# Linear attention and a GELU feed-forward on one core: the first batch by half its heads

## The chip, the cores and the metric

The kernel runs on one core of one Trainium2 chip. A core has TensorE (matmuls, results in PSUM), VectorE, ScalarE (activation functions), GpSimd (called POOL in profiles) and SyncE (SP, which issues most of the transfers here), and 16 DMA engines that move data between HBM and SBUF. The metric is the device time of one execution in microseconds (us); lower is better.

## The reference

Linear attention over 8 batches, 8 heads, 576 positions and head size 64, then a feed-forward layer on the heads put side by side (4608 tokens of 512):

```python
def phi(x):
    return np.where(x > 0, x, np.exp(x) - 1.0) + 1.0
q_p, k_p = phi(q), phi(k)
kv = np.einsum('bhsd,bhse->bhde', k_p, v)
z = np.sum(k_p, axis=2)
num = np.einsum('bhsd,bhde->bhse', q_p, kv)
den = np.einsum('bhsd,bhd->bhs', q_p, z)[..., None] + 1e-06
attn = num / den
# x = attn, transposed to (4608, 512)
h = x @ w_in                                  # 512 -> 2048
g = 0.5 * h * (1.0 + np.tanh(c * (h + 0.044715 * h * h * h)))
out = g @ w_out                               # 2048 -> 512
```

Inputs and the output are float32; the matmuls work in bf16.

## The kernel before

**Tiles.** Of each batch's 576 rows, 512 (`MAIN`) form one tile of tokens, in four chunks c of 128; the remaining 64 rows (`REST`) of all batches form a ninth tile, which is computed last. One iteration j computes one tile of 512 tokens: 16 blocks m of h (`h_mm`, four matmuls of 128x512 each, into one PSUM bank, then GELU on ScalarE into g), and the output in four chunks t, each of 16 matmuls in four groups u of four blocks m (`o_mm`). These are 32 slots, and a hand-written plan (`fill`, `at`, `run`) says after which slot of which iteration the work on a later batch stands. Iteration 0 goes through u in the outer loop, so that the quarters of w_out, which are still arriving, are needed one after the other: slots 16 to 19 need the first, 20 to 23 the second, 24 to 27 the third, 28 to 31 the fourth.

**Attention of one batch.** phi is max(x + 1, 1) ("linear", VectorE), limited by exp(x) (ScalarE; "least", a minimum on VectorE). v is cast into a tile with a column of ones behind each head (E = 65 columns), so that kv and z come from the same matmuls. Two heads make a block of kvbd, a block-diagonal tile of 128 rows and 130 columns. For each chunk of tokens, n = q_p times kvbd holds numerator and denominator; VectorE takes the reciprocal and multiplies, which gives x (`nab_evac`); x is transposed into xt. Batches 0 and 1 transpose on TensorE, later ones by DMA.

**The first batch** (`first_batch`, from line 377) stands ahead of iteration 0. Matmuls on a tile of zeros (`keep_warm`) fill TensorE's time during the loads. q is loaded in two halves by the parity of the head, k and v in halves of four heads (`halves`). Both halves of q, k and v go through phi and the casts, kv is computed in four banks and copied to kvbd by VectorE and ScalarE. Then each chunk c has n over all heads, in a pair of banks (`nab`, even chunks) or in two single banks (`nab_in_banks`, odd ones), the transpose, the copy of xt on ScalarE, and its quarter of the first three blocks m of h (`h_quarter`, 12 matmuls of 128x128). Block m = 3 follows as the first whole one.

**Batch 1** (`plan_second`) is woven into iteration 0: maps after slot 15, the transposes of q after 23, the casts of v after 25, kv after 26, then the n of its chunks after 27, 28, 29 and 30. In `kv`, VectorE first casts a part of the last quarter of w_out (line 484) and then copies kv into kvbd (line 290).

**Loads.** All loads of inputs and weights are issued by SP in one order: q, k, v of batch 0; the four pieces of w_in; then pieces of w_out and q, k, v of batch 1 in turn; then batch 2 (with the rest rows of k and v of batches 2 and 3, `load_rest`, line 118) and batch 3. Weights come as float32 and are cast to bf16, w_in and most of w_out by GpSimd. Loads use a pool of seven buffers (`pld`), and each transfer uses one of eight completion counters in turn, so a transfer is issued only when the eighth one before it has landed. PSUM has six single banks (`ps_b`) and one pair (`ps_a`).

```python
def load_w(wr, i):
    t = pld.tile([P, 4, 512], FP32, name="w_st", tag="ld")
    ...
    src = wr[:, :, 512 * i : 512 * (i + 1)] if wr is w_in_r else wr[:, 4 * i : 4 * i + 4, :]
    nc.sync.dma_start(out=t, in_=src)
```

A row of this piece of w_in is 512 float32, 2 KB in one run.

Of the kernel before, what the change touches and what calls it, by code (L numbers as in the profile page):

```python
# [15 lines left out]
def kernel(  # L16
# [6 lines left out]
    moe_w_out: bass.AP,  # L23
    out: bass.AP,
):

# [45 lines left out]
    def bank(name, shape, dt=FP32):  # L74
        return ps_b.tile(shape, dt, name=name, tag="b")
# [5 lines left out]

    ld = {}
    PAIRED = (0, 1)

    def ld_tile(name, b):
        shape = [P, NP, J * D] if b in PAIRED and name != "q" else [P, H, C * D]
# [3 lines left out]
        s = src[b].rearrange("h s d -> (h s d)").rearrange("(u n f) -> n u f", n=P, f=J * D)  # L90
        nc.sync.dma_start(out=ld[name, b][:, us, :], in_=s[:, us, :])  # L91

    def load_q_paired(b, parities=(0, 1)):
        src = q[b, :, 0:MAIN, :].rearrange("(u a) (p c) d -> p a u (c d)", a=2, c=C)
        for a in parities:
            nc.sync.dma_start(out=ld["q", b][:, NP * a : NP * (a + 1), :], in_=src[:, a])  # L96

    def load_main(name, src, b):
        ld_tile(name, b)
        nc.sync.dma_start(  # L100
            out=ld[name, b],
            in_=src[b, :, 0:MAIN, :].rearrange("h (p c) d -> p h (c d)", c=C),
        )

    def load_rest(name, src, m):
        t = (pqr if name == "qr" else prest).tile([P, H, D], FP32, name=name)
        ld[name, m] = t
        for s in range(2):
            r = t[REST * s : REST * (s + 1)]
            rows = src[2 * m + s, :, MAIN:S, :]  # L110
            if name == "qr" and m == 0:
                for a in range(2):
                    nc.sync.dma_start(
                        out=r[:, NP * a : NP * (a + 1), :],
                        in_=rows.rearrange("(u a) p d -> p a u d", a=2)[:, a],
                    )
            else:
                nc.sync.dma_start(out=r, in_=rows.rearrange("h p d -> p h d"))

# [10 lines left out]
    def load_w(wr, i):  # L130
        t = pld.tile([P, 4, 512], FP32, name="w_st", tag="ld")
        w_st[wr is w_in_r, i] = t
        src = wr[:, :, 512 * i : 512 * (i + 1)] if wr is w_in_r else wr[:, 4 * i : 4 * i + 4, :]
        nc.sync.dma_start(out=t, in_=src)

    def cast_w_in(i, fn, fs=slice(0, 512)):
        fn(
# [12 lines left out]
    for n in "qkv":  # L150
        ld_tile(n, 0)
    for s in range(2):
        load_q_paired(0, (s,))
        load_pairs("k", k, 0, halves[s])
    for s in range(2):
        load_pairs("v", v, 0, halves[s])
# [1 line left out]
        load_w(w_in_r, i)  # L158
    load_w(w_out_r, 0)
    ld_tile("q", 1)  # L160
    load_q_paired(1)
    load_w(w_out_r, 1)
    ld_tile("k", 1)
    load_pairs("k", k, 1)
# [127 lines left out]
    def nab_mm(qt_c, kvbd, ns, rows=slice(0, P)):  # L292
        for i in range(NP):
            nc.tensor.matmul(  # L294
                ns[i // 2][rows, 2 * E * (i % 2) : 2 * E * (i % 2 + 1)],
                lhsT=qt_c[:, i, rows],
                rhs=kvbd[:, i, :],
                skip_group_check=True,
            )

    def x_view(x, paired):
        return x.rearrange("p (u a d) -> p a u d" if paired else "p (a u d) -> p a u d", a=2, d=D)
# [16 lines left out]
        nab_mm(qt_c, kvbds[b % 4], [n_ps[:, a] for a in range(2)])  # L319
        return nab_evac(n_ps, b in PAIRED)  # L320

    def nab_in_banks(qt_c, b):
        ns = [bank("n_ps", [P, 4 * E]) for _ in range(2)]
        nab_mm(qt_c, kvbds[b % 4], ns)
        x = px.tile([P, d_model], BF16, name="x")
        for a in range(2):
            n_v = ns[a].rearrange("p (u e) -> p u e", e=E)
            r = psm.tile([P, NP], FP32, name="r1")
            nc.vector.reciprocal(r, n_v[:, :, D])
            nc.vector.tensor_tensor(  # L330
                x_view(x, b in PAIRED)[:, a],
                n_v[:, :, 0:D],
                r[:, :, None].to_broadcast([P, NP, D]),
                op=ALU.mult,
            )
        return x

    def transpose_x(x, xt_c, fn):
        t_ps = bank("t_ps", [P, NP, P], BF16)
        for i in range(NP):  # L340
            nc.tensor.transpose(t_ps[:, i, :], x[:, P * i : P * (i + 1)], ident)  # L341
        fn(out=xt_c, in_=t_ps)  # L342

    xts = {}
    qts = {}

    def h_mm(h_ps, xt, m, ts=slice(0, MAIN)):
        for c in range(KM):
            nc.tensor.matmul(  # L349
                h_ps[:, ts],  # L350
                lhsT=w_in_sb[:, c, P * m : P * (m + 1)],
                rhs=xt[:, c, ts],
                start=(c == 0),
                stop=(c == KM - 1),
                skip_group_check=True,
            )
# [20 lines left out]
    def first_batch():  # L377
        w_ps = bank("w_ps", [P, 512])

        def keep_warm(n):  # L380
            for _ in range(n):
                nc.tensor.matmul(w_ps, lhsT=warm[:, 0:P], rhs=warm)  # L382

        qt = pt.tile([P, C, NP, P], BF16, name="qt")
        qs = (slice(0, 4), slice(4, 8))

        def transpose_q(s, fn):
            t_ps = bank("t_ps", [P, C, 2, P], BF16)
            for i in range(2):
                for c in range(C):  # L390
                    h = 4 * s + 2 * i
                    nc.tensor.transpose(
                        t_ps[:, c, i, :], phi["q", 0][:, c, h : h + 2, :], ident
                    )
            fn(out=qt[:, :, 2 * s : 2 * s + 2, :], in_=t_ps)

        keep_warm(18)
        for s in range(2):
            for n, hs in (("q", qs[s]), ("k", halves[s])):
                exp_of(n, 0, hs)  # L400
                linear_of(n, 0, hs)
                least_of(n, 0, hs)
        transpose_q(0, nc.scalar.copy)
        keep_warm(10)
        transpose_q(1, nc.scalar.copy)
        keep_warm(2)
        for ii in range(2):
            cast_v_paired(0, halves[ii], nc.vector.tensor_copy)
        for ii in range(2):
            kv_ps = [bank("kv_ps", [P, E]) for _ in range(2)]  # L410
            kv_paired(0, ii, lambda a, ii: kv_ps[a])
            for a, fn in enumerate((nc.vector.tensor_copy, nc.scalar.copy)):
                block = slice(2 * a + ii, 2 * a + ii + 1)
                kv_evac(0, block, kv_ps[a].rearrange("p (i e) -> p i e", i=1), fn)
        gelu_table()
        for s in range(2):
            cast_w_in(0, nc.gpsimd.tensor_copy, slice(256 * s, 256 * s + 256))
        for i in range(1, 4):
            cast_w_in(i, nc.gpsimd.tensor_copy)
        for i in range(2):  # L420
            cast_w_out(i, nc.gpsimd.tensor_copy)
        cast_w_out(2, nc.gpsimd.tensor_copy, slice(0, 2))
        keep_warm(2)

        xts[0] = pt.tile([P, NP, MAIN], BF16, name="xt")
        x = {0: nab(qt[:, 0], 0), 1: nab_in_banks(qt[:, 1], 0)}
        for c in range(C):
            transpose_x(x[c], xt_chunk(0, c), nc.scalar.copy)
            if c + 2 < C:
                x[c + 2] = (nab, nab_in_banks)[c % 2](qt[:, c + 2], 0)  # L430
            if c > 0:
                h_quarter(0, c - 1, 3)
        h_quarter(0, C - 1, 3)

    first_batch()

# [311 lines left out]
```

## Time and profile before

| | us |
|---|---|
| Median of 3 runs | 287.87 (287.83 to 287.99) |
| The profiled execution | 288.24 |
| Its span, first to last instruction | 286.2 |
| ScalarE's time in table loads, 16 of them | 20.6 |
| TensorE, o matmuls (L642) | 126.3 |
| TensorE, h matmuls (L349, main tiles) | 116.7 |
| Load of w_in, issue to landing, median of 4 pieces | 14.7 |
| Load of w_out, issue to landing, median of 4 pieces | 13.6 |

The span is what the trace covers; the rest of the execution's time lies around it. "Busy" is the time in which an engine had an instruction at work. The granted clock of TensorE was 0.998 of full speed over the span. A timeline line has the start, the duration, the engine, the source line, the operation with output and input, the count and, in brackets, how long the engine had been idle and what released it. The two largest rows of TensorE make 243 of its 276.6 busy us, and a matmul of 128x512 is issued every 0.216 us in an unbroken stream: four of them, one block m of h, take 0.864 us.

### The profile page before, as it was taken

The page shows a single profiled execution, that of the slowest core. Times are in us where ns is not written, and L with a number is a line of the kernel's source. Part 1 is how long each engine was busy: PE and PEld are TensorE (multiplying, and loading weights), DVE is VectorE, ACT ScalarE, POOL GpSimd, SP SyncE. Part 2 cuts the span into 40 slices and gives each one's busy share as a digit, 9 for nine tenths or more (in the row PEclk, how much of TensorE's full clock was granted, in tenths as well). Part 3 has the DMA queues.
Part 4 walks back from the last instruction along what each step waited for, and adds up shares of the span by engine and source line. Part 5 has one row for each costly group of instructions (what it writes and reads, how often), then busy time and mean ns, then how long its engine had stood idle before and what let it go on. Part 6 is the DMA issues. An engine that isn't in the chain of part 4 may idle for free.

```text
span 286.2 us, 4541 instructions
## 1 busy us (share of the span) xinstructions
PE 276.6 (97%) x1839; PEld 137.1 (48%) x1868; DVE 107.8 (38%) x180; ACT 164.8 (58%) x226; POOL 18.4 (6%) x25
## 2 busy tenths in 40 slices
PE   8789999999999999999999999999999999999994
PEld 3464456445455445544554455444544444444443
DVE  3840476634865472544246614640412010000011
ACT  4766886795966934584458635763571275027400
POOL 5067230000000000000000000000000000000000
PEclk9999999999999999999999999999999999999999
DMA  7999999966989948935899489535131210120022
GB/s 249 409 405 397 410 400 264 342 243 188 151 238 310 275 133 220 349 77 147 220 315 182 95 238 359 84 103 153 37 39 49 88 49 0 60 89 0 0 73 73
DMA packets 71379, 53.76 MB, mean 188 GB/s; under 512 B 42048, under 2 KB 62784, under 8 KB 71360
## 3 DMA queue, kind: packets, MB, share of 16 engines
q1 hardware_dynamic: 68656, 44.58, 55.1%
q10 hardware_dynamic: 2704, 8.91, 8.9%
q8 instruction: 14, 0.23, 0.3%
q14 instruction: 5, 0.04, 0.0%
HBM read 36.70 MB, written 9.44 MB: 161 GB/s over the span
## 4 chain that ended last, share of the span: by engine, by line
PE 93%; DMA 3%; DVE 1%; issue 1%; SPq 1%; ACT 0%
PE o_ps L642 43%; PE h_ps L349 43%; PE n_ps L294 3%; DMA v_x<-in_v_dram 3%; PE kv_ps L278 1%; PE t_ps L341 1%; SPq L91 1%; PE kv_ps L263 0%; SPq L96 0%; PE t_ps L469 0%; DVE x L330 0%; DVE vp L241 0%; DVE x L309 0%; ACT xt L342 0%; PE w_ps L382 0%
## 5 line engine op out<-in xcount | busy, mean ns | idle before, releaser
L642 PE MATMUL o_ps<-w_out_sb,g 128*128 128x512 bf16 (+1 forms) x581 | 126.3, 373 | 0.8 <-issue 0.2
L349 PE MATMUL h_ps<-xt,w_in_sb 128*128 128x512 bf16 (+1 forms) x556 | 116.7, 356 | 1.1 <-ACT xt L342 0.2
L359 ACT ACTIVATE g<-h_ps 128x512 bf16<-128x512 f32 x144 | 84.9, 597 | 46.5 <-PE h_ps L349 42.3
L642 PEld LDWEIGHTS <-g 128*128 128x128 bf16 x592 | 57.5, 98 | 65.2 <-issue 0.2
L349 PEld LDWEIGHTS <-w_in_sb 128*128 128x128 bf16 x636 | 57.5, 98 | 59.5 <-issue 0.7
L608 ACT COPY o_sb<-o_ps 128x512 f32<-128x512 f32 (+1 forms) x19 | 10.9, 574 | 61.3 <-PE o_ps L642 54.2
L608 DVE COPY o_sb<-o_ps 128x512 f32<-128x512 f32 (+1 forms) x18 | 12.1, 674 | 69.0 <-PE o_ps L642 69.0
L307 DVE RECIPROCAL r<-n_ps 128x8 f32<-128x8 f32 x34 | 7.1, 207 | 50.6 <-PE n_ps L294 50.6
L309 DVE TENSOR_TENSOR x<-n_ps,r 128x512 bf16<-128x512 f32 x34 | 23.5, 691 | 1.2
L212 ACT ACTIVATE q_e<-q_x 128x2048 bf16<-128x2048 f32 (+1 forms) x9 | 15.5, 1721 | 2.9 <-DMA q_x<-in_q_dram 2.8
L212 ACT ACTIVATE k_e<-k_x 128x2048 bf16<-128x2048 f32 (+2 forms) x9 | 15.8, 1755 | 0.8 <-DMA k_x<-in_k_dram 0.8
L236 DVE TENSOR_TENSOR q_p<-q_p,q_e 128x2048 bf16<-128x2048 bf16 (+1 forms) x9 | 9.9, 1105 | 15.9 <-ACT q_e L212 15.8
L223 DVE TENSOR_SCALAR q_p<-q_x 128x2048 bf16<-128x2048 f32 (+1 forms) x9 | 10.0, 1106 | 14.3 <-DMA q_x<-in_q_dram 14.3
L349 PE MATMUL h_ps<-xt_rest,w_in_sb 128*128 128x512 bf16 x63 | 13.9, 379 | 0.1
L294 PEld LDWEIGHTS <-qt 128*128 128x128 bf16 x128 | 9.7, 98 | 7.2 <-DVE x L309 1.0
L294 PE MATMUL n_ps<-kvbd,qt 128*128 128x130 bf16 x128 | 12.7, 221 | 0.0
L223 DVE TENSOR_SCALAR k_p<-k_x 128x2048 bf16<-128x2048 f32 (+2 forms) x9 | 10.2, 1133 | 5.6 <-DMA k_x<-in_k_dram 5.6
L236 DVE TENSOR_TENSOR k_p<-k_p,k_e 128x2048 bf16<-128x2048 bf16 (+2 forms) x9 | 11.0, 1227 | 0.8 <-ACT k_e L212 0.6
L382 PE MATMUL w_ps<-warm 128*128 128x512 bf16 x31 | 9.3, 454 | 1.3 <-DVE warm L177 1.2
L373 ACT ACT_TABLE_LOAD x8 | 10.3, 1283 | 0.1
L212 ACT ACT_TABLE_LOAD x8 | 10.3, 1283 | 0.1
L290 DVE CAST kvbd<-kv_ps 64x260 bf16<-64x260 f32 (+2 forms) x18 | 6.6, 365 | 8.5 <-PE kv_ps L278 8.2
(49 smaller groups left out, 94.5 us busy)
## 6 DMA issues: line engine op xcount, KB each, us to landing
out_dram<-o_sb ACTq DMA_DIRECT2D x16, 512.0 KB, 3.4
q_x<-in_q_dram SPq DMA_DIRECT2D x6, 1024.0 KB, 7.3
k_x<-in_k_dram SPq DMA_DIRECT2D x6, 1024.0 KB, 11.0
v_x<-in_v_dram SPq DMA_DIRECT2D x6, 1024.0 KB, 6.7
w_st<-in_moe_w_in_dram SPq DMA_DIRECT2D x4, 1024.0 KB, 14.7
w_st<-in_moe_w_out_dram SPq DMA_DIRECT2D x4, 1024.0 KB, 13.6
q_x<-in_q_dram SPq DMA_DIRECT2D x4, 512.0 KB, 8.6
k_x<-in_k_dram SPq DMA_DIRECT2D x2, 576.0 KB, 5.6
```

What stands on the lines that cost most here:

```text
L212: nc.scalar.activation(by_chunk(exps[name, b], hs), x[:, hs].rearrange("p h (c d) -> p h c d", d=D), AF.Exp,)
L223: nc.vector.tensor_scalar(by_chunk(phi[name, b], hs), x[:, hs].rearrange("p h (c d) -> p h c d", d=D), 1.0, 1.0, op0=ALU.add, op1=ALU.max,)
L236: nc.vector.tensor_tensor(p, p, e, op=ALU.min)
L294: nc.tensor.matmul(ns[i // 2][rows, 2 * E * (i % 2) : 2 * E * (i % 2 + 1)], lhsT=qt_c[:, i, rows], rhs=kvbd[:, i, :], skip_group_check=True,)
L307: nc.vector.reciprocal(r, n_v[:, :, :, D])
L309: nc.vector.tensor_tensor(x_view(x, paired), n_v[:, :, :, 0:D], r[:, :, :, None].to_broadcast([P, 2, NP, D]), op=ALU.mult,)
L349: nc.tensor.matmul(h_ps[:, ts], lhsT=w_in_sb[:, c, P * m : P * (m + 1)], rhs=xt[:, c, ts], start=(c == 0), stop=(c == KM - 1), skip_group_ ...
L359: nc.scalar.activation(g[:, m, :], h_ps, AF.Gelu_apprx_tanh)
L373: nc.scalar.preload_act_table_set("gelu_apprx_tanh_and_others")
L382: nc.tensor.matmul(w_ps, lhsT=warm[:, 0:P], rhs=warm)
L608: (nc.scalar.copy if on_scalar else nc.vector.tensor_copy)(dst, src)
L642: nc.tensor.matmul(o_ps, lhsT=g[:, m, P * t : P * (t + 1)], rhs=w_out_sb[:, m, fs], start=(m == 0), stop=(m == MM - 1),)
```

## The change

q of batch 0 is loaded by head instead of by parity: heads 0 to 3 first, in an order that puts heads 0 and 2 ahead of 1 and 3, in two transfers each half. The first batch then runs in two halves of four heads. Half ii has its own kv (in the pair of banks, copied by ScalarE alone), n (two matmuls of 128x130 in one bank), reciprocal and multiply, transpose (two blocks) and copy of xt. x's half gives two of the four blocks over which h is summed, so h of m = 0 and 1 begins with the first half as a partial sum; m = 2 and 3 get the first half as one matmul of 512 columns for each block after the fourth chunk; the second half adds to all four, which stay in four banks. The order of VectorE and ScalarE is changed: v's first half is cast ahead of the last minimum of k, and the copies of q's transposes stand between the exps. w_in is loaded in eight pieces of 256 columns, and cast in pieces of 128 columns (the first quarter) and 256 columns. The rest rows of k and v of batches 2 and 3 are loaded in two transfers each, of unequal size.

```diff
+    SPLITS = {"kr": (60, 56), "vr": (52, 44)}
...
-    def load_q_paired(b, parities=(0, 1)):
-        src = q[b, :, 0:MAIN, :].rearrange("(u a) (p c) d -> p a u (c d)", a=2, c=C)
-        for a in parities:
-            nc.sync.dma_start(out=ld["q", b][:, NP * a : NP * (a + 1), :], in_=src[:, a])
+    def main_rows(src, b, hs=slice(0, H)):
+        return src[b, hs, 0:MAIN, :].rearrange("h (p c) d -> p h (c d)", c=C)
+
+    def load_q_heads(b, to, hs):
+        rows = main_rows(q, b, hs)
+        nc.sync.dma_start(out=ld["q", b][:, to : to + rows.shape[1], :], in_=rows)
...
+            elif m == 1 and name in SPLITS:
+                n = SPLITS[name][s]
+                for ps in (slice(0, n), slice(n, REST)):
+                    nc.sync.dma_start(out=r[ps], in_=rows[:, ps].rearrange("h p d -> p h d"))
...
-        src = wr[:, :, 512 * i : 512 * (i + 1)] if wr is w_in_r else wr[:, 4 * i : 4 * i + 4, :]
-        nc.sync.dma_start(out=t, in_=src)
+        if wr is w_in_r:
+            for f in range(0, 512, 256):
+                nc.sync.dma_start(
+                    out=t[:, :, f : f + 256], in_=wr[:, :, 512 * i + f : 512 * i + f + 256]
+                )
+        else:
+            nc.sync.dma_start(out=t, in_=wr[:, 4 * i : 4 * i + 4, :])
...
     for s in range(2):
-        load_q_paired(0, (s,))
+        for a in range(2):
+            load_q_heads(0, 4 * s + 2 * a, slice(4 * s + a, 4 * s + a + 3, 2))
         load_pairs("k", k, 0, halves[s])
...
-    load_q_paired(1)
+    for a in range(2):
+        load_q_heads(1, 4 * a, slice(a, H, 2))
...
+    def nab_half(n_ps, x, qt_c, ii):
+        for a in range(2):
+            nc.tensor.matmul(
+                n_ps[:, 2 * E * a : 2 * E * (a + 1)],
+                lhsT=qt_c[:, 2 * a + ii, :],
+                rhs=kvbds[0][:, 2 * a + ii, :],
+                skip_group_check=True,
+            )
+        n_v = n_ps[:, 0 : 4 * E].rearrange("p (a s e) -> p a s e", a=2, e=E)
+        r = psm.tile([P, 2, 2], FP32, name="r1")
+        nc.vector.reciprocal(r, n_v[:, :, :, D])
+        nc.vector.tensor_tensor(
+            x[:, 4 * D * ii : 4 * D * (ii + 1)].rearrange("p (s a d) -> p a s d", a=2, d=D),
+            n_v[:, :, :, 0:D],
+            r[:, :, :, None].to_broadcast([P, 2, 2, D]),
+            op=ALU.mult,
+        )
...
         keep_warm(18)
-        for s in range(2):
-            for n, hs in (("q", qs[s]), ("k", halves[s])):
-                exp_of(n, 0, hs)
-                linear_of(n, 0, hs)
-                least_of(n, 0, hs)
-        transpose_q(0, nc.scalar.copy)
-        keep_warm(10)
-        transpose_q(1, nc.scalar.copy)
+        exp_of("q", 0, qs[0])
+        linear_of("q", 0, qs[0])
+        least_of("q", 0, qs[0])
+        exp_of("k", 0, halves[0])
+        linear_of("k", 0, halves[0])
+        least_of("k", 0, halves[0])
+        exp_of("q", 0, qs[1])
+        transpose_q(0)
+        keep_warm(8)
+        linear_of("q", 0, qs[1])
+        least_of("q", 0, qs[1])
+        exp_of("k", 0, halves[1])
+        transpose_q(1)
         keep_warm(2)
-        for ii in range(2):
-            cast_v_paired(0, halves[ii], nc.vector.tensor_copy)
-        for ii in range(2):
-            kv_ps = [bank("kv_ps", [P, E]) for _ in range(2)]
-            kv_paired(0, ii, lambda a, ii: kv_ps[a])
-            for a, fn in enumerate((nc.vector.tensor_copy, nc.scalar.copy)):
-                block = slice(2 * a + ii, 2 * a + ii + 1)
-                kv_evac(0, block, kv_ps[a].rearrange("p (i e) -> p i e", i=1), fn)
+        linear_of("k", 0, halves[1])
+        cast_v_paired(0, halves[0], nc.vector.tensor_copy)
+        least_of("k", 0, halves[1])
+        cast_v_paired(0, halves[1], nc.vector.tensor_copy)
+        kv_copies(0, kv(0))
         gelu_table()
-        for s in range(2):
-            cast_w_in(0, nc.gpsimd.tensor_copy, slice(256 * s, 256 * s + 256))
+        keep_warm(1)
+        for m in range(4):
+            cast_w_in(0, nc.gpsimd.tensor_copy, slice(P * m, P * (m + 1)))
         for i in range(1, 4):
-            cast_w_in(i, nc.gpsimd.tensor_copy)
+            for f in range(0, 512, 256):
+                cast_w_in(i, nc.gpsimd.tensor_copy, slice(f, f + 256))
...
-        keep_warm(2)
-
-        xts[0] = pt.tile([P, NP, MAIN], BF16, name="xt")
-        x = {0: nab(qt[:, 0], 0), 1: nab_in_banks(qt[:, 1], 0)}
-        for c in range(C):
-            transpose_x(x[c], xt_chunk(0, c), nc.scalar.copy)
-            if c + 2 < C:
-                x[c + 2] = (nab, nab_in_banks)[c % 2](qt[:, c + 2], 0)
-            if c > 0:
-                h_quarter(0, c - 1, 3)
-        h_quarter(0, C - 1, 3)
+        steps = [(c, ii) for ii in range(2) for c in range(C)]
...
+        def nab_step(i):
+            c, ii = steps[i]
+            n_ps = pair_of_banks("n_ps")[:, 0] if i % 2 and i > 2 else bank("n_ps", [P, 4 * E])
+            nab_half(n_ps, xs[c], qt[:, c], ii)
+
+        def h_part(c, ii):
+            ts = slice(P * c, P * (c + 1))
+            for m in range(4 if ii else 2):
+                if (c, ii) == (0, 0):
+                    hs[m] = bank("h_ps", [P, MAIN])
+                h_mm(hs[m], xt, m, ts, range(2 * ii, 2 * ii + 2), c == 0)
+
+        nab_step(0)
+        nab_step(1)
+        kv_ps = kv(1)
+        for i, (c, ii) in enumerate(steps):
+            transpose_x(xs[c], xt_chunk(0, c), nc.scalar.copy, blocks[ii])
+            if i == 0:
+                kv_copies(1, kv_ps)
+            if i + 2 < len(steps):
+                nab_step(i + 2)
+            if i > 0:
+                h_part(*steps[i - 1])
+            if i == 4:
+                for m in (2, 3):
+                    hs[m] = bank("h_ps", [P, MAIN])
+                    h_mm(hs[m], xt, m, blocks=range(2))
+        h_part(*steps[-1])
```

`kv(ii)` computes half ii's kv into the pair of banks, and `kv_copies` copies it into kvbd with two ScalarE copies of 64x130.

## The prediction

> **What bounds the kernel now.** I read the page first, then the windows by stage, then the timelines of GpSimd, VectorE and TensorE where an engine waited for a load.
>
> ```profile
> span 286.2 us, 4541 instructions
> PE 276.6 (97%) x1839; PEld 137.1 (48%) x1868; DVE 107.8 (38%) x180; ACT 164.8 (58%) x226; POOL 18.4 (6%) x25
> ```
>
> TensorE is busy 97% of the span. The windows say where the rest is:
>
> ```profile
> core 0: us, PE busy (x) PEld busy (x) DVE busy (x) ACT busy (x) POOL busy (x), PEclk, DMA share, GB/s
> 0.00:11.60 11.60, 9.46 (x47) 4.25 (x47) 6.53 (x10) 7.33 (x7) 4.06 (x16) 1.00 0.85 310
> 11.60:16.40 4.80, 2.99 (x97) 2.33 (x99) 3.94 (x13) 2.91 (x7) 2.02 (x2) 1.00 1.06 411
> 16.40:20.60 4.20, 4.14 (x64) 3.60 (x62) 1.39 (x5) 2.87 (x6) 1.89 (x1) 1.00 1.04 401
> 20.60:31.00 10.40, 10.35 (x49) 4.72 (x49) 1.23 (x1) 7.52 (x13) 5.68 (x3) 1.00 1.06 402
> 31.00:41.50 10.50, 10.45 (x65) 5.13 (x68) 6.06 (x5) 10.07 (x8) 3.45 (x2) 1.00 1.05 406
> 41.50:50.50 9.00, 8.52 (x148) 5.62 (x150) 5.83 (x13) 5.24 (x11) 1.29 (x1) 1.00 0.94 286
> ```
>
> TensorE's real gap is in the start, up to 16.4 us. But see the last two columns: until 41.5 us the DMA engines are full, at 401 to 411 GB/s. So TensorE is busy and the loads are full at once, and the loads may be just as close to setting the pace. The timelines show who waits for the loads (start, duration, then the idle time and its releaser in brackets):
>
> ```profile
> 14.32 2.02 POOL L137 CAST w_in_sb<-w_st 128x1024 bf16<-128x1024 f32 x2 [9.55 <-DMA w_st<-in_moe_w_in_dram]
> ...
> 36.67 1.56 POOL L143 CAST w_out_sb<-w_st 128x1024 bf16<-128x1024 f32 x1 [3.58 <-DMA w_st<-in_moe_w_out_dram]
> 42.06 1.29 POOL L143 CAST w_out_sb<-w_st 128x1024 bf16<-128x1024 f32 x1 [3.83 <-DMA w_st<-in_moe_w_out_dram]
> ```
> ```profile
> 42.03 0.43 DVE L143 CAST w_out_sb<-w_st 128x512 bf16<-128x512 f32 x1 [1.79 <-DMA w_st<-in_moe_w_out_dram]
> 42.38 0.59 DVE L290 CAST kvbd<-kv_ps 64x130 bf16<-64x130 f32 x2
> ```
> ```profile
> 43.03 0.40 PE L294 MATMUL n_ps<-kvbd,qt 128*128 128x130 bf16 x4
> 43.26 1.14 PE L642 MATMUL o_ps<-w_out_sb,g 128*128 128x512 bf16 x4
> 44.45 0.23 PE L294 MATMUL n_ps<-kvbd,qt 128*128 128x130 bf16 x1
> ```
>
> This is the place that decides. The last w_out piece lands at 42.03. VectorE has waited 1.79 us for it; only then, in its order, come its cast and the two copies of batch 1's kv (L290), which end at 42.97. The first n of batch 1 needs them and starts at 43.03, and TensorE, working without a gap, reaches it at 43.03 too. Slack on either side: none. The next n (44.45) waits for the x of the first (its weight load sat idle 0.54 us for VectorE's x), so the chain n, x, n follows the landing rigidly. After 50.5 us TensorE is busy 98.87 of 99.50 us and waits for no load.
>
> **What the Trainium skill says.** "DMA: Bandwidth & Descriptors", Why small descriptors are slow: a packet carries a fixed cost of about 3 cycles beside its 32-byte beats. By that a 2 KB piece costs 67 cycles and two 1 KB pieces 70, 4.5% more (an estimate from the page). The trace agrees: 2 KB pieces moved at 408 GB/s from 12 to 24 us, 1 KB pieces (q and k of batch 2) at 387 from 40.5 to 45 us:
>
> ```profile
> DMA packets 2458, 4.90 MB, mean 408 GB/s; under 512 B 69, under 2 KB 91, under 8 KB 2456
> ```
> ```profile
> DMA packets 1691, 1.74 MB, mean 387 GB/s; under 512 B 18, under 2 KB 1664, under 8 KB 1691
> ```
>
> Same page, Why a DMA increments its semaphore by 16 and not by 1: a transfer runs on the largest number of engines up to 16 that divides both outer sizes, the lowest-numbered ones, and has landed when the last is done. So parts of 60, 56, 52 and 44 rows leave out the highest engines; no view here shows single engines. "TensorE: Matmul & The Clock Gate", Part 1: an idle window of some 3.4 us halves TensorE's clock; here it is 1.00 in every window.
>
> **The change, part by part.**
>
> (a) Start of the first batch. q now comes with heads 0 to 3 first, in two loads of 256 KB. An issue costs SP about 0.5 us and 256 KB need 0.65 us at 391 GB/s, so the stream doesn't run dry: cost 0 to 0.2 us. The first v half, by the spacing of about 1.4 us between landings (q 4.59, k 5.98, q 7.35, k 8.83, second v 11.66), is there near 10.25. VectorE casts it before the last min of k: to 11.0 instead of 11.55. kv of the first half then ends at 11.6, its two ScalarE copies (0.54 like the pair at 42.37) at 12.2, then the table load (1.28) to 13.5, which the first n and x cover. VectorE casts v's second half to 12.6. Eight half steps follow: reciprocal and multiply of one half come every 0.55 us (TT starts 14.95 and 15.50), so 4.4 us if nothing else waits. Two things do: the fourth step takes the double bank that the second kv holds until its copies end, about 14.6; and the two whole matmul groups of m 2 and 3 (4 x 0.216 = 0.86 us) stand ahead of the sixth transpose. I find the last multiply at 18.2 to 18.65, plus transpose and copy (0.32 + 0.38 estimated as two thirds of 0.58) and 8 matmuls of 56 ns: m 0 to 3 are done at 19.5 to 20.0. Before: the 12 groups after them take 12 x 0.864 = 10.37 us and end at 30.96, so 20.6. TensorE is early by 0.6 to 1.1 us; I take 0.8. Bounds: minus 0.7 if the clock drops, 1.3 at best.
>
> (b) w_in by halves. 4.19 MB go from 2 KB to 1 KB pieces: 10.28 us at 408 GB/s, 10.84 at 387, 10.95 at 383 (mean by bytes of the trace's four 1 KB stretches: 391, 382, 372, 387), 11.27 at 372. All that stands behind it in the queue lands later by d = 0.56 to 0.99 us; I take 0.65. Six more completions (four of w_in, two of q) are in that. Below nothing: w_in's first piece lands 0.6 us after its bytes would be through on average (4.46 MB by 13.7, summing the DMA view's slices), the second 2.1 us after (5.51 MB by 16.3; it lands at 18.36), so some engine falls 1.5 us behind; shorter queues might shrink that, bound -1.5. The eight completion counters and SP's longer wait cost nothing: at least 2 MB stay queued. The casts by halves start sooner; GpSimd needs 0.5 us for each m, TensorE 0.86, so it keeps ahead.
>
> (c) Rest rows in parts. Four more issues by SP behind the last w_out, each 1.3 us at the rate of vr's. v of batch 2 and q, k of batch 3 stand behind them. VectorE's cast of v starts at 52.79 and afterwards it idles 5.36 us before 60.17: that covers it, cost 0; beyond 5 us it would show.
>
> (d) What meets what. Stage by stage, the loads later by 0.65 and TensorE earlier by 0.8:
> - w_out 0: cast done 27.95 + 0.65, wanted 30.16: fine.
> - w_out 1: 33.09 + 0.65 = 33.74, wanted 33.6: waits 0.1.
> - w_out 2: 38.23 + 0.65 = 38.88, wanted from 38.0: start 38.9 against 38.76 before. The 0.8 is gone here.
> - w_out 3: lands 42.68, cast to 43.03, copies to 43.62, first n at 43.68 instead of 43.03; second n 45.10 instead of 44.45. The whole 0.65 stays, since TensorE has no idle time left after it.
>
> Sum: profiled 288.24 (span 286.2 and 2.04 around it) + 0.65 = 288.89; on the median of the runs, 287.87, it gives 288.5.
>
> **Rivals.**
> 1. The 1 KB pieces cost nothing here (the stream is held by one late engine, not by packets). Then w_out 3 lands at 42.03, TensorE's lead dies there all the same, and the time is 287.9. For it: the first q and k stretches differ little by eye. Against: four separate 1 KB stretches are all slower.
> 2. Faster: the halved pieces keep the late engine from falling 1.5 us behind. One place, the landing of w_out 3; it decides once that is earlier than 42.03. With 1.5 - 0.65 = 0.85 us earlier and TensorE's lead of 0.8, 287.1. For it: w_in 0 shows no such lag. Against: nothing says that depth makes it.
> 3. The start itself is late: ScalarE's table load, the double bank or a halved clock delay m 0 to 3 past 20.6 + 0.65, by up to 0.7 more than that: 289.2. For it: ScalarE and VectorE are the chain there, TensorE only 62% busy; against: 1.3 us of room.
>
> That the halves don't take effect is excluded by the order of instructions: the first h comes before the second half's n.
>
> **How the numbers follow.** Forecast 0.56 (its own range 288.2 to 288.9), rival 1 0.16, rival 2 0.14, rival 3 0.14. The bound of 0.2% is 0.58 us, about what can be told from no change: 288.45. Some 0.17 of the forecast lies below it. Slower 0.39 + 0.14 = 0.53; same 0.16 + 0.17 = 0.33; faster 0.14. Range: 287.4 to 289.1, leaving out about a tenth at each end.
>
> **What would show it.** Right: w_in's stretch at 380 to 390 GB/s; VectorE's first w_out 3 cast near 42.7; the first n of batch 1 near 43.7; TensorE idle for about 1.4 us between 30 and 43.7 us, where it was busy; m 4 started near 19.8. Wrong: that cast at or before 42.0, or w_in at 405 GB/s, or h groups starting after 20.6.

## The result, and the profile after

The changed kernel takes 292.94 us (median of 6 runs, 291.96 to 293.40) against 287.94 us for the kernel before in the same runs: a ratio of 1.017, 95% interval 1.0154 to 1.0186, so 5 us slower. The direction was foreseen, the size was not. The profiled execution took 292.92 us, its span grew by 4.9 us. From the page of the kernel after:

```profile
span 291.1 us, 4590 instructions
PE 278.5 (96%) x1865; PEld 136.6 (47%) x1865; DVE 107.8 (37%) x180; ACT 165.0 (57%) x230; POOL 19.7 (7%) x30
```

The same stages as before, by windows (busy time of TensorE, its weight loads, VectorE, ScalarE and GpSimd with counts; then clock, DMA share, GB/s):

```profile
0.00:11.60 11.60, 8.57 (x44) 3.81 (x44) 5.53 (x9) 6.43 (x7) 4.50 (x16) 1.00 0.81 280
11.60:16.40 4.80, 3.04 (x97) 2.19 (x97) 4.10 (x11) 4.07 (x10) 1.93 (x4) 1.00 1.08 386
16.40:20.60 4.20, 4.13 (x58) 3.30 (x56) 2.40 (x9) 2.14 (x6) 2.36 (x3) 1.00 1.09 382
20.60:31.00 10.40, 10.40 (x55) 4.96 (x55) 0.67 (x1) 8.07 (x15) 6.18 (x6) 1.00 1.07 396
31.00:41.50 10.50, 9.95 (x59) 4.89 (x57) 6.22 (x6) 9.74 (x9) 3.45 (x2) 1.00 1.05 410
41.50:50.50 9.00, 8.45 (x134) 4.82 (x132) 4.74 (x12) 5.41 (x10) 1.30 (x1) 1.00 0.89 290
```

w_in (second and third line) comes at 382 to 386 GB/s instead of 401 to 411, as foreseen. But the first line has 280 instead of 310 GB/s, ahead of nearly all of w_in: a loss that was not foreseen. The place that decided before, on VectorE's timeline and on TensorE's:

```profile
43.68 0.43 DVE L153 CAST w_out_sb<-w_st 128x512 bf16<-128x512 f32 x1 [1.78 <-DMA w_st<-in_moe_w_out_dram]
44.02 0.59 DVE L302 CAST kvbd<-kv_ps 64x130 bf16<-64x130 f32 x2
```
```profile
44.66 0.40 PE L306 MATMUL n_ps<-kvbd,qt 128*128 128x130 bf16 x4 [0.39 <-DVE kvbd L302]
...
46.09 0.41 PE L306 MATMUL n_ps<-kvbd,qt 128*128 128x130 bf16 x4 [0.17 <-DVE x L321]
```

The last w_out piece is cast at 43.68 instead of 42.03, and the two n follow at 44.66 and 46.09 instead of 43.03 and 44.45. The delay passes on whole, as the prediction had it, only it is 1.64 us and not 0.65. That is a third of the loss. The other 3.3 us arise after 50 us, where the kernel before had almost no idle time. ScalarE's timeline, first of the kernel before, then of the kernel after (ACTq is the issue of a DMA):

```profile
50.98 1.62 ACT L359 ACTIVATE g<-h_ps 128x512 bf16<-128x512 f32 x3 [0.53 <-PE h_ps L349]
52.01 0.87 ACTq L633 DMA_DIRECT2D out_dram<-o_sb  x2
52.93 0.60 ACT L359 ACTIVATE g<-h_ps 128x512 bf16<-128x512 f32 x1 [0.33 <-PE h_ps L349]
...
56.93 1.28 ACT L212 ACT_TABLE_LOAD   x1
58.23 1.91 ACT L212 ACTIVATE q_e<-q_x 128x2048 bf16<-128x2048 f32 x1
```
```profile
52.60 1.62 ACT L375 ACTIVATE g<-h_ps 128x512 bf16<-128x512 f32 x3 [0.53 <-PE h_ps L365]
53.64 5.63 ACTq L688 DMA_DIRECT2D out_dram<-o_sb  x2
59.31 2.56 ACT L375 ACTIVATE g<-h_ps 128x512 bf16<-128x512 f32 x5 [5.09 <-DVE vr L267]
61.89 1.28 ACT L224 ACT_TABLE_LOAD   x1
63.18 1.91 ACT L224 ACTIVATE q_e<-q_x 128x2048 bf16<-128x2048 f32 x1
```

Up to the third gelu everything is 1.6 us late. Then ScalarE issues its first two stores of the output. Before, both issues took 0.87 us; now they take 5.63 us, the first one alone 5.15. ScalarE works in order, so it stands idle for 5.09 us ahead of its next gelu, where it had stood idle for 0.33. (The releaser in the bracket is VectorE only because its event came last in time; ScalarE was held by its own issue.) The exp of batch 2 starts at 63.18 instead of 58.23. TensorE feels it at three places. Its timeline, first before, then after:

```profile
56.12 7.07 PE L642 MATMUL o_ps<-w_out_sb,g 128*128 128x512 bf16 x32
63.02 1.03 PE L349 MATMUL h_ps<-xt,w_in_sb 128*128 128x512 bf16 x4
63.98 0.32 PE L278 MATMUL kv_ps<-vp,k_p 128*64 128x65 bf16 x8
```
```profile
57.75 0.81 PE L697 MATMUL o_ps<-w_out_sb,g 128*128 128x512 bf16 x3
59.97 6.43 PE L697 MATMUL o_ps<-w_out_sb,g 128*128 128x512 bf16 x29 [1.41 <-ACT g L375]
66.24 1.03 PE L365 MATMUL h_ps<-xt,w_in_sb 128*128 128x512 bf16 x4
68.20 0.32 PE L290 MATMUL kv_ps<-vp,k_p 128*64 128x65 bf16 x8 [0.94 <-DVE k_p L248]
...
83.70 2.75 PE L365 MATMUL h_ps<-xt,w_in_sb 128*128 128x512 bf16 x12 [0.47 <-DMA xt<-x]
```

The o group began at 56.12 before and at 57.75 now, 1.63 late; the h group after it at 63.02 and 66.24, 3.22 late; kv of batch 2 at 63.98 and 68.20, 4.22 late; the end 4.9 late. So there are two losses, one at the start and one at ScalarE's store, and the experiments had to find the cause of each.

### The profile page after: what moved, and what is told of

It reads as the page before. It is cut to its first block, busy times and chain, and to the rows that moved or that the text cites. A ratio compares the mean times of both kernels' runs of the same rounds, so it can differ in the third digit from the quotient of the medians.

```text
span 291.1 us, 4590 instructions
## 1 busy us (share of the span) xinstructions
PE 278.5 (96%) x1865; PEld 136.6 (47%) x1865; DVE 107.8 (37%) x180; ACT 165.0 (57%) x230; POOL 19.7 (7%) x30
## 4 chain that ended last, share of the span: by engine, by line
PE 75%; DMA 11%; SPq 4%; ACT 3%; DVE 2%; ACTq 2%; issue 1%; POOL 0%
PE h_ps L365 36%; PE o_ps L697 34%; DMA w_st<-in_moe_w_out_dram 5%; DMA w_st<-in_moe_w_in_dram 3%; SPq L140 3%; PE n_ps L306 3%; DMA k_x<-in_k_dram 2%; ACTq L688 2%; PE kv_ps L290 2%; ACT g L375 1%; DMA xt<-x 1%; ACT q_e L224 1%; ACT k_e L224 1%; SPq L144 1%; SPq L93 1%
## 5 line engine op out<-in xcount | busy, mean ns | idle before, releaser
L365 PE MATMUL h_ps<-xt,w_in_sb 128*128 128x512 bf16 (+1 forms) x572 | 118.6, 356 | 0.7 <-DMA xt<-x 0.5
L321 DVE TENSOR_TENSOR x<-n_ps,r 128x512 bf16<-128x512 f32 x32 | 22.1, 691 | 1.1
L306 PEld LDWEIGHTS <-qt 128*128 128x128 bf16 x112 | 8.6, 98 | 7.5 <-DVE x L321 1.1
L306 PE MATMUL n_ps<-kvbd,qt 128*128 128x130 bf16 x112 | 11.1, 221 | 0.6 <-DVE kvbd L302 0.4
L147 POOL CAST w_in_sb<-w_st 128x1024 bf16<-128x1024 f32 (+1 forms) x10 | 8.6, 869 | 12.2 <-DMA w_st<-in_moe_w_in_dram 12.1
L259 DVE CAST vp<-v_x 128x2048 bf16<-128x2048 f32 x6 | 7.3, 1224 | 5.5 <-DMA v_x<-in_v_dram 5.5
```

The source lines that it names most:

```text
L147: fn(out=w_in_sb[:, :, 512 * i + fs.start : 512 * i + fs.stop], in_=w_st[True, i][:, :, fs],)
L306: nc.tensor.matmul(ns[i // 2][rows, 2 * E * (i % 2) : 2 * E * (i % 2 + 1)], lhsT=qt_c[:, i, rows], rhs=kvbd[:, i, :], skip_group_check=True,)
L321: nc.vector.tensor_tensor(x_view(x, paired), n_v[:, :, :, 0:D], r[:, :, :, None].to_broadcast([P, 2, NP, D]), op=ALU.mult,)
L365: nc.tensor.matmul(h_ps[:, ts], lhsT=w_in_sb[:, c, P * m : P * (m + 1)], rhs=xt[:, c, ts], start=(start and c == 0), stop=(c == KM - 1), s ...
```

## The experiments

Ratios are against the kernel before, measured beside each run; the cast and the stop are read from each run's one profiled execution. "Stop" is an issue of ScalarE's first store that takes over 3 us.

| Run | us | Ratio, interval | Last w_out cast | Stop |
|---|---|---|---|---|
| changed kernel | 292.94 | 1.017 (1.0154 to 1.0186) | 43.68 | 5.15 us |
| 1 rest rows equal | 292.86 | 1.0166 (1.0149 to 1.0184) | 43.85 | 4.46 us |
| 2 before + parts | 287.79 | 1.0001 (0.9991 to 1.0011) | 41.96 | no |
| 3 before + w_in halves | 288.30 | 1.0015 (1.0008 to 1.0022) | 42.52 | no |
| 4 before + q in four | 289.83 | 1.0072 (1.0045 to 1.0098) | 43.37 | no |
| 5 before + 3 and 4 | 290.75 | 1.008 (1.0062 to 1.0097) | 42.8 | no |
| 6 new computation, w_in whole | 293.44 | 1.0187 (1.0166 to 1.0207) | 43.6 | 4.35 us |
| 7 changed, store later | 289.85 | 1.0054 (1.0035 to 1.0073) | 44.8 | no |
| 8 as 6, k first | 292.63 | 1.0151 (1.0132 to 1.0169) | 42.5 | 4.80 us |
| 9 before + five copies, new tile | 293.25 | 1.0171 (1.0154 to 1.0188) | 44.6 | 4.72 us |
| 10 changed, kv copies on VectorE | 290.45 | 1.0079 (1.0062 to 1.0096) | 44.4 | no |
| 11 meant to beat both | 290.39 | 1.0075 (1.005 to 1.0099) | 44.9 | no |
| 12 changed, batch 3 later | 299.31 | 1.0395 (1.0368 to 1.0423) | 43.5 | 3.51 us |
| 13 before + two copies, new tile | 290.61 | 1.0093 (1.0077 to 1.011) | 44.3 | no |
| 14 before + six woven, new tile | 290.87 | 1.0104 (1.0089 to 1.0119) | 44.4 | no |
| 15 before + five copies | 290.97 | 1.0095 (1.0078 to 1.0112) | 42.1 | 5.12 us |
| 16 before + six woven | 288.15 | 0.9996 (0.9985 to 1.0007) | 41.9 | no |
| 17 changed + six copies | 290.33 | 1.007 (1.0055 to 1.0086) | 44.3 | no |

**One part at a time (runs 1 to 4).** Run 1 is the changed kernel without the parts of the rest rows; the others are the kernel before with one part.

```diff
-    SPLITS = {"kr": (60, 56), "vr": (52, 44)}
+    SPLITS = {}
```

> The changed kernel with the rest rows of batches 2 and 3 loaded in one transfer each, as before. Theory (three costs of the loads add up: q in four transfers, w_in in 1 KB pieces, rest rows in unequal parts): the last w_out piece still lands near 43.65 us, but v of batch 2 is cast near 54 us instead of 56.4, ScalarE's store issue near 54 us takes about 0.9 us instead of 5.6, no wait of TensorE on GELU, and the time falls by about 3.3 us to 289.6 us. Rival (the late store follows from everything being 1.6 us later, whatever the rest rows' shape): the issue still takes 4 to 5 us and the time stays near 292.5 us.

> The kernel before with only the rest rows of batches 2 and 3 in unequal parts. Theory: nothing changes up to 44 us, then ScalarE's first store issue takes some 5 us and the time rises by 2 to 3.3 us, to 290 to 291.2 us. Rival: 287.9 us, since the parts alone cost nothing.

> The kernel before with only w_in loaded in eight pieces of 1 KB rows (casts as before). Theory: 4.2 MB at 387 instead of 408 GB/s, the last w_out piece is cast by VectorE at 42.6 instead of 42.03 us, and the time rises by the same 0.56 us to 288.5 us. Rival (the start's order of work is what costs, not the loads): 287.9 us.

> The kernel before with only q of batch 0 in four transfers of 256 KB instead of two of 512 KB, in the same order of bytes. Theory: the stream runs thin between 3.5 and 5.5 us (below 270 GB/s instead of about 400), v's second half lands 1.0 to 1.3 us later, near 12.8 us, the last w_out piece near 43.1 us, and the time rises by about 1.05 us to 289.0 us. Rival (the gap in the stream came from elsewhere in the changed start, such as the order of loads of heads): 287.9 us.

Taking the parts out saves nothing that can be measured and leaves the stop, and putting them in alone costs nothing. So the first theory, that the parts made the second loss, fell. w_in in halves costs about what was foreseen: cast 0.49 us later, time up by 0.3. q in four loads costs 1.34 us at the cast; the time rose by 1.8 us in the median and the span of the profiled execution by 1.3. The windows show where, first of the kernel before, then of run 4:

```profile
3.50:4.00 0.50, 0.50 (x3) 0.15 (x1) 0.00 (x0) 0.00 (x0) 0.44 (x3) 1.00 1.09 391
4.00:4.50 0.50, 0.50 (x2) 0.15 (x1) 0.00 (x0) 0.00 (x0) 0.50 (x2) 1.00 1.10 424
4.50:5.00 0.50, 0.50 (x2) 0.15 (x1) 0.41 (x1) 0.41 (x1) 0.22 (x2) 1.00 1.00 396
```
```profile
3.50:4.00 0.50, 0.50 (x3) 0.15 (x1) 0.00 (x0) 0.00 (x0) 0.44 (x3) 1.00 0.85 151
4.00:4.50 0.50, 0.50 (x2) 0.15 (x1) 0.27 (x1) 0.29 (x1) 0.50 (x2) 1.00 0.79 134
4.50:5.00 0.50, 0.50 (x2) 0.15 (x1) 0.50 (x1) 0.50 (x1) 0.44 (x2) 1.00 0.69 198
```

The last column falls from about 400 to 134 to 198 GB/s for 1.5 us: some 0.36 MB, 0.9 us at 404 GB/s, are not moved there, and 0.05 MB more are missing up to 6 us, together about 1.0 of the 1.34 us. The changed kernel has the same gap (150, 138, 184 GB/s); its depth differs between profiles, with 337, 304 and 290 GB/s in run 6, where it lasts longer. What all share is the landing of the second half of v, the last load of batch 0: 12.91 to 13.80 us in the nine programs that load q in four and ahead of k, 11.54 to 11.99 in the five with q in two loads and the load buffers of the kernel before, run 11 apart (12.31). It also delays the start: in run 4 TensorE's first o stands at 32.34 instead of 30.96 us.

**Is the stop made by late loads? (runs 5, 6, 7)** None of the parts alone brought the stop. Run 5 has both load changes of runs 3 and 4 on the old computation; run 6 the new computation with q still in four loads, w_in whole and equal rest rows; run 7 the changed kernel with the store moved:

```diff
-                at(1, 2, store)
+                at(1, 12, store)
```

> The kernel before with q of batch 0 in four loads and w_in in halves, the computation of the first batch unchanged. Theory A (ScalarE's stop at its first store comes from how late the loads are when the store is issued, whoever made them late): the last w_out cast stands near 43.8 us, the store issue blocks ScalarE for 4 to 5 us, and the time is 292 to 293 us. Theory B (the stop belongs to what the new computation changes: which load buffer comes free when, and so which loads of batch 2 stand in SP's queue ahead of the store): no stop, the store issue takes about 1 us, and the time is 289.7 to 290.3 us (287.9 plus 1.34 and 0.49).

> The changed kernel with w_in in whole pieces and the rest rows in equal parts: the new computation of the first batch and the four loads of q alone. Theory A: the last w_out cast near 43.2 us, as late as with q in four loads alone, where ScalarE did not stop; so no stop here and 289.2 us. Theory B: the stop of 4 to 5 us is there, and the time is 292 to 292.6 us.

> The changed kernel with ScalarE's first two stores issued ten slots later (after slot 12 of iteration 1 instead of slot 2), nothing else. If the blocked issue makes the second part of the loss: no idle time of TensorE over 0.4 us between 50 and 70 us, and 289.6 to 290.0 us. If the loss there has another cause (the loads of batch 2 themselves late): 291.5 to 293 us.

Theory A fell both ways: late loads without the new computation do not stop, the new computation without the other parts does. (The loads of run 5 were less late than meant, 42.80 instead of 43.8 at the cast, but run 13 below has its cast at 44.28 and no stop. In run 5 the first n came at 44.47 all the same, since TensorE, without a gap, had started its o at 32.34.) In run 5 SP issued q and k of batch 3 at 49.83 and 50.46 us and the store came at 53.45; in run 6 at 49.81, 50.53 and 53.57. These times agree within 0.12 us, and yet one stops and the other doesn't. Run 7 shows what the stop is worth: without it the ratio is 1.0054 instead of 1.017, 3.3 us, the whole second loss. Its profile agrees: the first n of batch 1 is 2.72 us late there, the span 2.7 us longer, and from 50 to 90 us TensorE has no idle time over 0.23 us.

**k first (run 8).** As run 6, with each half of k issued ahead of the two loads of q, and phi of k and q in that order.

> The changed kernel with w_in whole and the rest rows in equal parts, and each half of k issued ahead of the two loads of q (phi of k then comes ahead of phi of q). If the stream runs dry because small transfers come with nothing queued ahead of them: the rate from 3.5 to 5.5 us is near 390 GB/s, the last w_out cast stands at 42.0 to 42.5 us instead of 43.2, and the time is about 1 us below that of the same kernel with q first: 287.8 to 288.3 us without a stop of ScalarE, 291 to 291.5 with it. If small transfers cost the same wherever they stand: cast near 43.2, no gain.

Half right: the cast comes at 42.5 instead of 43.6, but the rate from 3.5 to 5.5 us is 374, 368, 303 and 259 GB/s against 337, 304, 290 and 311 in run 6, so the gap has moved more than shrunk. The second half of v lands at 12.66 instead of 13.19 us (11.63 before). The stop stays, and the first n comes no earlier (44.77 against 44.59), since TensorE starts its o later (32.70). The time is above what was expected with a stop.

**Is it the place in ScalarE's instructions? (runs 9, 10)** Counting ScalarE's instructions in the built programs, waits included, the first store stood at place 61 or 63 in all kernels so far without the stop, run 7 with its moved store apart, and at 66 or 67 in all with it. Run 9 adds only this to the kernel before, where ScalarE is idle:

```diff
+        spare = const.tile([P, 1], BF16, name="spare")
+        for _ in range(5):
+            nc.scalar.copy(out=spare, in_=warm[:, 0:1])
         keep_warm(18)
```

Run 10 turns `nc.scalar.copy` into `nc.vector.tensor_copy` in `kv_copies` of the changed kernel.

> The kernel before with five copies of one column on ScalarE ahead of the first batch, where ScalarE has nothing to do, and nothing else changed: they move its first store from place 61 to place 66 of ScalarE's instructions, and leave its time as it was. In the runs so far ScalarE never stopped where that store stood at place 61 or 63, and stopped where it stood at 66 or 67. Theory C (the place in ScalarE's stream of instructions decides, by an instruction fetch that comes between): the store issue blocks ScalarE for 4 to 5 us, and the time is 290.5 to 291.5 us, with loads and computation of the kernel before. Theory D (something of the new computation other than that place decides, its buffers or its timing): store issue of 0.9 us, and 287.9 to 288.3 us.

> The changed kernel with the four copies of kv of the first batch on VectorE instead of ScalarE, nothing else: the first store moves from place 67 to place 62 of ScalarE's instructions, at the same time or up to 0.5 us later. Theory C: no stop at the store, and 289.7 to 290.5 us, as with the store ten slots later. Theory D: the stop of about 5 us stays, and 292.5 to 293.5 us.

As to the stop, both came as theory C said: one in run 9, none in run 10. But run 9 was 2 us slower than the stop explains.

**A version meant to beat both (run 11).**

> A version meant to beat both: the changed kernel with each half of q in one load of 512 KB (the order of the heads is made by exp and by the linear part, each in two instructions), w_in in whole pieces, the rest rows in equal parts, the store ten slots later, and VectorE's cast of the last w_out quarter behind the copies of kv of batch 1. By theory no gap in the stream, the last w_out landing near 42.0 us as before, no stop at the store, and the first n of batch 1 up to 0.5 us ahead of 43.03: 287.4 to 287.9 us. If the stream or the start is late all the same: 288.5 us or more.

It did not. There is no gap in the stream (411 and 418 GB/s at 4 to 5 us), no stop and no wait for the last w_out. But TensorE's clock was 0.86 from 12 to 24 us in the profile, the last quarter of m 0 to 3 began only at 21.54, and the first n of batch 1 came at 44.97. TensorE's start decides there. No run was faster than the kernel before by more than its interval.

**Copies apart from their tile (runs 12 to 17).** Run 13 is run 9 with two copies, run 14 has six copies in slots 27 to 31 of iteration 0. Runs 15 and 16 repeat 9 and 14 with the output `xt_rest[:, 0, 0:1]` instead of a new tile. Run 17 adds six such copies at the start of the changed kernel. Run 12 loads q and k of batch 3 behind the transposes of batch 2.

> The changed kernel with q and k of batch 3 loaded together with its v, behind the transposes of batch 2, instead of ahead of the store: when the store is issued, 1 MB (v of batch 2) stands in the DMA engines instead of 2 to 3 MB. The store keeps place 67 of ScalarE's instructions. Theory E (the store waits for an instruction fetch of ScalarE, and the fetch waits behind the loads that are queued in the DMA engines): the store issue still blocks, but for 1 to 3 us instead of 5.1, and ends soon after v of batch 2 is through, by 56.5 us. If the length of the stop has nothing to do with the queued loads: 4.5 us or more again. The time itself says less, since batch 3 comes later.

> The kernel before with two copies of one column on ScalarE ahead of the first batch: the first store stands at place 63 instead of 61. Theory C: no stop, store issue of 0.9 us, and 287.9 to 288.4 us. If it is the copies themselves, not the place, that made the run with five of them slow: 1 us or more above the kernel before.

> The kernel before with six copies of one column on ScalarE between slots 27 and 31 of iteration 0, where ScalarE waits for TensorE, and none ahead of the first batch: the first store stands at place 66, and start and loads are those of the kernel before. Theory C: the stop of 4 to 5 us at the store and 291 to 291.8 us (3.0 to 3.5 us for the stop, up to 0.3 for the copies). Without it: 288.0 to 288.4 us.

> Five copies of one column ahead of the first batch in the kernel before, as once already, but written into a tile that exists (a column of xt of the rest rows, which is overwritten later), so that no new tile moves the load buffers by 32 bytes. The first store stands at place 66. Theory C (the place decides): the stop of 4 to 5 us at the store, the load rate of the kernel before (about 408 GB/s from 12 to 24 us), and 291.0 to 291.5 us. If the new tile made the stop: no stop, and 287.9 to 288.3 us.

> Six copies of one column woven between slots 27 and 31 of iteration 0 in the kernel before, written into the same existing tile, store at place 66. With the new tile this kernel did not stop at the store, against theory C. If that was because of the lower load rate: the stop is there now, 291.0 to 291.6 us. If the place alone does not decide: no stop, and 288.0 to 288.5 us.

> The changed kernel with six copies of one column on ScalarE ahead of the first batch, written into the same existing tile: the first store moves from place 67 to place 73. If what stops the store is an instruction fetch that is asked for at a fixed place near 64: six instructions of 0.2 us each at the start do not let it finish much earlier, so the stop is there, perhaps up to 1 us shorter, 292 to 293 us. If a stop needs the store within about four places of the limit: no stop, 289.5 to 290 us.

Run 15 isolates the stop: loads and start are those of the kernel before, and everything is on time until the store. It has the old computation too, so theories B and D, which laid the stop to the new one, fell. ScalarE's timeline, and below it the DMA view of run 15 from 55.3 to 55.4 us (queue, packets, MB, share of the engines):

```profile
2.03 1.10 ACT L398 COPY xt_rest<-warm 128x1 bf16<-128x1 bf16 x5
...
50.99 1.62 ACT L359 ACTIVATE g<-h_ps 128x512 bf16<-128x512 f32 x3 [0.53 <-PE h_ps L349]
52.03 5.60 ACTq L635 DMA_DIRECT2D out_dram<-o_sb  x2
57.68 2.56 ACT L359 ACTIVATE g<-h_ps 128x512 bf16<-128x512 f32 x5 [5.06 <-issue]
```
```profile
q14 instruction: 1, 0.01, 19.6%
```

In run 16 the store stands at the same place 66, at nearly the same time, with the same loads, and does not stop. Its ScalarE timeline, and its DMA view from 46.2 to 46.4 us:

```profile
52.48 0.87 ACTq L633 DMA_DIRECT2D out_dram<-o_sb  x2
53.40 0.60 ACT L359 ACTIVATE g<-h_ps 128x512 bf16<-128x512 f32 x1 [0.32 <-PE h_ps L349]
```
```profile
q14 instruction: 1, 0.01, 17.0%
```

So theory C fell as it stood: the place alone doesn't decide (runs 14 and 16), and a place further back need not stop (run 17, place 73). Runs 14 and 16 differ from run 15 in one thing more: their first store carries no semaphore wait, as every store that was held does. The wait itself is not the hold: it is for a copy into o_sb, and in the changed kernel ScalarE's copies into o_sb ended at 48.20 us, long before the issue at 53.64. But place 66 or 67 together with such a wait would fit every run here, and was not tested.

What also goes with the stop is an 8 KB fetch of instructions. In each of the seven runs with a stop one such packet starts 1.67 to 2.00 us ahead of the end of the blocked issue: at 57.05 with the end at 58.79 in the changed kernel, at 55.33 with the end at 57.15 in run 15. (In the changed kernel and in runs 8, 12 and 15 a second packet starts during the hold, so this pairing was made after the fact.) In runs 10, 14, 16 and 17 a fetch came already at 46.3 to 48.6 us, ahead of v of batch 2 and the loads of batch 3; in run 7 the fetches (56.3 and 57.9) came ahead of the moved store (60.95), as they did in run 11; and in the kernels with the store at place 61 or 63 they came 1.9 us or more after it had begun. "Runtime: NRT & Kernel Launch", Instruction fetch mechanics, in the Trainium skill says that an engine's sequencer fetches its instructions in blocks through a DMA queue of its own, and that the cost is mostly hidden. The traces agree that blocks come by DMA (8 KB here, 16 KB on the other instruction queue, where the page has 16 KB); that the held store waited for one is not shown, since no run moved a fetch alone. Run 12 fits a fetch that waits behind loads only in part: with 1 MB queued the stop is 3.51 us instead of 5.15, but it ends at 57.15, later than expected, and from 56 to 57 us the DMA engines move nothing while the issue is still held. Its time, 299.31 us, comes from batch 3: TensorE waits 6.98 us for its xt. The trace doesn't say which engine a fetch belongs to, and what sets its moment stayed open.

The other loss of runs 9, 13 and 14 goes with their new tile. It moved all load buffers, and the working tiles behind them, by 32 bytes, the load buffers from a multiple of 64 to 32 past one. The windows of the kernel before and of run 13, 12 to 24 and 24 to 40 us:

```profile
12.00:24.00 12.00, 10.13 (x148) 7.10 (x138) 4.99 (x17) 8.31 (x16) 6.45 (x5) 1.00 1.06 408
24.00:40.00 16.00, 15.89 (x85) 7.74 (x86) 7.05 (x6) 13.35 (x15) 6.59 (x4) 1.00 1.05 404
```
```profile
12.00:24.00 12.00, 10.07 (x172) 7.10 (x159) 5.33 (x17) 8.08 (x17) 5.81 (x4) 1.00 1.04 386
24.00:40.00 16.00, 15.45 (x84) 7.32 (x82) 5.19 (x5) 13.10 (x15) 7.13 (x4) 1.00 1.06 381
```

408 and 404 GB/s become 386 and 381 with the same transfers, and the last w_out cast moves from 42.03 to 44.3. With the buffers where they were (run 16) the rate is 406 and the time that of the kernel before. Run 13 shows it cleanly; in the profiles of runs 9 and 14 the rate is 386 as well, but TensorE's clock was also 0.72 from 12 to 24 us, and its late start (first o at 33.71 and 33.48) decides the first n. That the load buffers' place, and not that of another moved tile, sets the rate was not tested apart.

## Why the prediction was wrong

- **(a) "so the stream doesn't run dry: cost 0 to 0.2 us": this step failed.** The time to issue and the time to move the bytes were compared as averages over the 16 engines. In the changed kernel the engines' parts of the first k half, which stands behind the two small loads, land from 5.5 to 7.0 us; before, from 5.6 to 6.0. While some engines have not begun, the stream is thin. The first half of v, foreseen near 10.25 us, landed at 11.42. Measured: 1.34 us at the last w_out cast (run 4). That it comes from small loads with nothing queued ahead is shown only in part: with k ahead of them (run 8) v's second half was 1.0 us late instead of 1.6 (run 6). How the engines get to start apart stays open.
- **(a) "TensorE is early by 0.6 to 1.1 us": failed with it.** The second half of q reached exp at 8.68 instead of 7.35 us, and TensorE waited 1.81 us for it. Counted back from the first o at 31.31 (12 groups of 0.864 us), m 4 started at 20.94 instead of 20.6: late by 0.35. There was no lead to lose. Rival 3 had a late start, but from ScalarE, banks or clock and not from the loads. The clock was 1.00 in this profile, though 0.72 from 12 to 24 us in those of runs 7, 10 and 17; and other profiles of the new computation start later at a clock of 1.00 (first o at 32.12 in run 1, 32.45 in run 6). So how late the start is changes from one execution to the next.
- **(b) right in the main.** 387 GB/s against a foreseen 383 to 387, and 0.49 us at the cast when done alone, a little under the 0.56 to 0.99 foreseen (0.65 taken). Rival 1, that it costs nothing, is out by run 3's interval.
- **(c) right**: 1.0001 alone (run 2). VectorE waited 2.25 us for v of batch 2 there, and its idle time covered it.
- **(d) right in its mechanism, wrong in its input.** The landing of the last w_out passes whole to the first n and the second n: 1.65 us in, 1.63 and 1.64 out. The term was 0.65; it should have had q in it, 1.34 alone. The two parts don't simply add: alone they give 0.49 and 1.34, together 0.77 on the old computation (run 5) and 1.65 in the changed kernel. The parts of the landing show one reason. Before, 14 of the 16 engines had landed the last w_out by 40.62 us, the last two at 41.82 and 42.01; in run 4 one engine was 1.2 us behind the rest, in run 5 none. So a late engine, as rival 2 has it, can set the landing that decides. w_in in halves alone (run 3) did not remove the lag (two engines 1.3 us behind), and what sets it was not tested.
- **What the sum had no term for:** the step ended at "TensorE has no idle time left after it" and took the rest as a mere shift. ScalarE's first store turned from 0.87 into 5.63 us of issue, worth 3.3 us (run 7; 3.2 us of span in run 15). None of the rivals had it, and why the issue is held stays open. The four copies of kv and the halved copies of xt were priced by duration; that they change ScalarE's stream of instructions ahead of its first DMA was not considered. Nothing in the profile before shows this price, but it shows a ScalarE that issues DMAs between gelus that TensorE waits for, and an issue there could have been bounded from above.

## What to carry to other kernels

Before a stream's first large load, don't split small loads further on the strength of averages: look at the rate in slices of half a microsecond, and judge the loss where the last load lands. When a change leaves an unexplained shift late in the kernel, look for an issue row (ACTq, SPq) whose mean has grown: an engine that computes and issues DMAs stops computing while an issue is held. In an experiment that adds a tile, see that it doesn't move the other buffers, or it measures two things.

## What the runs showed of the hardware that was not expected

- The first DMA issue on ScalarE was held for 3.5 to 5.15 us in seven programs and took 0.38 to 0.39 us in the twelve others, though the only thing it has to wait for is ScalarE's own copy, which had ended long before. Five copies of one column ahead of everything else were enough (run 15: 290.97 us against 288.15).
- With the load buffers at 32 bytes past a multiple of 64 (and the tiles behind them moved too): 381 to 386 GB/s instead of 404 to 408. No other offset was tried. In the Trainium skill "DMA: Bandwidth & Descriptors", How a descriptor splits into AXI transactions, describes extra beats for reads that don't start at 256 bytes; here the reads were unchanged and the place in SBUF moved, which the page doesn't price.
- Two loads of 256 KB in place of one of 512 KB at the head of the stream: 134 to 198 GB/s for 1.5 us (run 4), and the last load of the batch 1.3 us or more later in all nine programs that have them ahead of k.
- One or two of the 16 engines can be 1.2 to 1.4 us behind the rest with their part of a 1 MB load, and the wait ends only with them: 41.82 and 42.01 us for the last w_out before, where 14 had landed by 40.62.
